# Forward stage of a fused attention and FFN training step: the 64-row part of the products as two 32-row matmuls beside score pairs, and a queue and bank of their own for weight-gradient sums

## The chip, the cores and the metric

One core of one Trainium2 chip runs the whole program in one launch. The metric is the device time of the program in microseconds; the time before is the median of three runs. Instructions of each engine run in their program order: TensorE (matmuls and their weight loads), VectorE, ScalarE, GpSimd and SyncE, the last two also issuing most of the DMAs. What one engine needs of another is waited for by semaphores.

## The reference

A layer of attention and a SwiGLU FFN side by side on the same normalised input, forward, and the gradients of all inputs but one. S = 2048 rows, D = 448, 16 heads of 28, F = 1792, bf16 inputs, batch 1.

```python
def _A_ref(x, wqkv, wo):
    qkv = (x @ wqkv).reshape(B, S, 3, H, Dh).transpose(2, 0, 3, 1, 4)
    q, k, v = qkv[0], qkv[1], qkv[2]
    scores = jnp.einsum("bhqd,bhkd->bhqk", q, k) * (Dh ** -0.5)
    p = _softmax(scores, axis=-1)
    o = jnp.einsum("bhqk,bhkd->bhqd", p, v)
    return o.transpose(0, 2, 1, 3).reshape(B, S, D) @ wo

def _B_ref(x, w_gate, w_up, w_down):
    return (_silu(x @ w_gate) * (x @ w_up)) @ w_down

xn = _layernorm(x, axis=-1)
return x + _A_ref(xn, A_wqkv, A_wo) + _B_ref(xn, B_w_gate, B_w_up, B_w_down)
# outputs: this, and its vjp with grad_out for x and the five weights
```

## The kernel before

It has a prologue, a forward loop, a backward loop and an end.

The prologue normalises x into xn_sp (rows on partitions), transposes it into xnT (four chunks of D on partitions: 128, 128, 128 and 64 rows, the last filled up with zeros), and makes q, k and v of head group 0 (proj_unit, four matmuls each into one bank, evicted with a constant added that sets the spare head columns).

The forward loop has 256 steps (g, qc, kt): head group g of four heads of 32 padded rows, query chunk qc of 512, key tile kt of 128. A step (L517 to L544) has two halves. Each half makes the scores of two heads with two 32-row matmuls into s_ps (L531), at row positions 0 and 32 in the first half, 64 and 96 in the second, and ScalarE takes their exponential into eT (L535). In the second half the four PV matmuls of the step before follow (L511). After each half fill() puts other work of the forward stage on TensorE, from one queue of jobs; pace is what is left in the queue over the steps left, and a half gets 0.45 or 0.55 of it. The costs in the queue are set by hand (MM, MMD).

The queue holds, for each of 14 blocks fc of 128 columns of F and each quarter sc of the rows: the gate product a, the up product u, and dh, the gradient of the product's input, four 512-column matmuls each (L339) into one bank of ps_f. After a ScalarE takes a tanh (L349) and VectorE makes g1 and, in two operations, w (L351 to L356); after u VectorE makes two products (L363, L365) and after dh two more (L373). These go as fT by DMA to hd_d (GpSimd, L378) and transposed into f_sp (SyncE, L375). Between u and dh of the next block stand the three weight-gradient sums of the block before (dW_items, L313): 16 matmuls of 448 columns each into one bank, evicted by VectorE (L319, L323). Other jobs are put at the front of the queue: the projections of the next head group, the layouts of q and k (sp_layouts), and after each (g, qc) o_items: o_raw is copied out by VectorE (L423), transposed on TensorE (tr, L432), scaled (L437 to L440), then dO is made by 16 small matmuls (do, L454) and evicted with its row sums (L461 to L473); after the last qc follow the 16 matmuls of dWo (L400).

All of these take their banks from ps_f, which has three; scores have four and PV one, eight in all. fT has three buffers, f_sp two. weight_layout (L250) transposes weights for backward through the one buffer sp_stage. At step 224 GpSimd issues the load of w_down into the buffer W (load_w, L493), which the projection weights wq_sb share until then.

The backward loop (L772) and the end are not edited. In backward, scores and their gradients are pairs of 32-row matmuls at rows 0 and 32 (L793) and at 64 and 96 (L803), VectorE multiplies (L814) and ScalarE takes exponentials (L808).

Of the kernel before, what the change touches and what calls it, by code (L numbers as in the profile page):

```python
# [37 lines left out]
def kernel(  # L38
# [72 lines left out]
    ps_f = bst.enter_context(tc.tile_pool(name="ps_f", bufs=3, space=PSUM))  # L111
# [15 lines left out]
    pool.memset(xn_sp[:, :, D:], 0.0)  # L127
    pool.memset(wq_sb, 0.0)
    for c, (d0, dn) in enumerate(DCH):
        pool.tensor_copy(  # L130
            out=wq_sb[:dn, c].rearrange("p t g (hh r) -> p t (g hh) r", r=HP)[:, :, :, :DH],
            in_=wst[:dn, c, :].rearrange("p (t h d) -> p t h d", t=3, h=H))
    sp.dma_start(out=dy_sp[:, :, :D], in_=dy_d)
    pool.memset(dy_sp[:, :, D:], 0.0)
# [13 lines left out]
    def proj_unit(g, tq, sc, evac):  # L148

        key = (g, tq)  # L150
        if sc == 0:
            qk_tiles[key] = (vp if tq == 2 else qkp).tile([P, S], BF16, name=("qT", "kT", "vT")[tq])
        dst = qk_tiles[key]
        pp = ps_f.tile([P, 512], FP32, name="f_ps")

        def mm(c):
            pe.matmul(pp[:], lhsT=wq_sb[:, c, tq, g, :], rhs=xnT[:, 4 * sc:4 * sc + 4, c, :],  # L157
                      start=(c == 0), stop=(c == 3))
            if c < 3:
                return  # L160
            o = dst[:, sc * 512:(sc + 1) * 512]
            if tq == 0:
                if evac == "act":
                    act.copy(out=o, in_=pp[:])
                else:
                    dve.tensor_copy(out=o, in_=pp[:])
            elif evac == "act":
                act.activation(out=o, in_=pp[:], func=ACT.Identity, bias=r_ones[:, 0:1], scale=1.0)
            else:
                dve.tensor_scalar(out=o, in0=pp[:], scalar1=r_ones[:, 0:1], scalar2=None, op0=ALU.add)  # L170
        return mm
# [18 lines left out]
    for b in range(5):  # L190
        if b < 4:
# [7 lines left out]
            for i in range(4):  # L199
# [3 lines left out]
                                  op0=ALU.subtract, op1=ALU.mult)  # L203
                pt = ps_s.tile([P, 4, P], BF16, name="s_ps")
# [3 lines left out]
        if b > 0:  # L208
            for tq in range(3):
                m = proj_unit(0, tq, b - 1, "act" if tq == 0 else "dve")  # L210
                for c in range(4):
                    m(c)
    proj_done(0)
# [12 lines left out]
    for w in wgu:  # L226
        pool.memset(w[64:, :, 3, :], 0.0)
    pool.memset(wd3[:, :, 64:], 0.0)
# [3 lines left out]
    def load_ffn_w(fc):  # L232
        w, fs = wgu[fc % 2], slice(fc * P, (fc + 1) * P)
        q = sp if fc < 2 else pool
        for i, src in enumerate((B_w_gate, B_w_up)):
            q.dma_start(out=w[:, i, 0:3, :], in_=src[0:384, fs].rearrange("(c p) f -> p c f", p=P))
            q.dma_start(out=w[:64, i, 3, :], in_=src[384:448, fs])
# [3 lines left out]
    sp.dma_start(out=wd3[:, :, 0:64], in_=B_w_down[:, 384:448].rearrange("(fc p) d -> p fc d", p=P))  # L241
# [20 lines left out]
    queue = deque()  # L262
    cur = deque()
    left = [0.0]

    def fill(budget):

        while budget > 0.05:
            if not cur:
                if not queue:  # L270
                    return
                cur.extend(queue.popleft())
            cost, fn = cur.popleft()
            fn()
            budget -= cost
            left[0] -= cost

    def push(jobs, front=False):
        left[0] += sum(c for job in jobs for c, _ in job)
        if front:  # L280
            queue.extendleft(reversed(jobs))
        else:
            queue.extend(jobs)

    def proj_items(g):
        out = []
        for tq in range(3):
            for sc in range(4):
                box = {}

                def go(c, tq=tq, sc=sc, box=box):
                    if c == 0:
                        box["m"] = proj_unit(g, tq, sc, "dve")
                    box["m"](c)
                out.append([(MM, lambda c=c, go=go: go(c)) for c in range(4)])
        out.append([(0.0, lambda: proj_done(g))])
        return out

    ffn = {}

    def dW_items(fc):

        out = []
        for wi in range(3):
            box = {}

            def go(t, wi=wi, box=box):
                src = ffn[fc]
                if t == 0:
                    box["ps"] = ps_f.tile([P, 512], FP32, name="f_ps")  # L310
# [4 lines left out]
                if t < NT - 1:  # L315
                    return
                if wi == 0:
# [14 lines left out]
    def ffn_items(fc, sc, extra):  # L332
# [3 lines left out]
        def mm(name, w, src, c):  # L336
            if c == 0:
                st[name] = ps_f.tile([P, 512], FP32, name="f_ps")
            pe.matmul(st[name][:], lhsT=w(c), rhs=src[:, tsl, c, :], start=(c == 0), stop=(c == 3))  # L339

        def a(c):
            if c == 0 and sc == 0:
                ffn[fc] = spp.tile([P, 3 * NT, P], BF16, name="f_sp")
                if fc + 1 < NFC:
                    load_ffn_w(fc + 1)
            mm("a", lambda c: wgu[fc % 2][:, 0, c, :], xnT, c)
            if c == 3:
                t_sb = st["t"] = ftmp.tile([P, 512], FP32, name="t_sb")
                act.activation(out=t_sb[:], in_=st["a"][:], func=ACT.Tanh, scale=0.5)  # L349
                g1 = st["g1"] = ftmp.tile([P, 512], FP32, name="g1")  # L350
                dve.scalar_tensor_tensor(out=g1[:], in0=t_sb[:], scalar=1.0, in1=st["a"][:],  # L351
                                         op0=ALU.add, op1=ALU.mult)
                w = st["w"] = ftmp.tile([P, 512], FP32, name="w_sb")
                dve.scalar_tensor_tensor(out=w[:], in0=t_sb[:], scalar=1.0, in1=g1[:],
                                         op0=ALU.subtract, op1=ALU.mult)
                dve.scalar_tensor_tensor(out=w[:], in0=w[:], scalar=-0.5, in1=t_sb[:],  # L356
                                         op0=ALU.mult, op1=ALU.add)

        def u(c):
            mm("u", lambda c: wgu[fc % 2][:, 1, c, :], xnT, c)  # L360
            if c == 3:
                o = st["o"] = fT.tile([P, 3, 512], BF16, name="fT")
                dve.scalar_tensor_tensor(out=o[:, 0, :], in0=st["g1"][:], scalar=0.5, in1=st["u"][:],  # L363
                                         op0=ALU.mult, op1=ALU.mult)
                dve.scalar_tensor_tensor(out=st["w"][:], in0=st["w"][:], scalar=1.0, in1=st["u"][:],  # L365
                                         op0=ALU.add, op1=ALU.mult)

        def dh(c):
            mm("dh", lambda c: wdT[fc % 2][:, c, :], dyT, c)
            if c == 3:  # L370
                o = st["o"]
                for wi, src in ((2, "g1"), (1, "w")):
                    dve.scalar_tensor_tensor(out=o[:, wi, :], in0=st["dh"][:], scalar=0.5, in1=st[src][:],  # L373
                                             op0=ALU.mult, op1=ALU.mult)
                sp.dma_start_transpose(out=ffn[fc][:, 12 * sc:12 * sc + 12, :],  # L375
                                       in_=o[:].rearrange("p w s -> p (w s)"))
                for wi in range(3):
                    pool.dma_start(out=hd_d[tsl, :, G + NFC * wi + fc, :].rearrange("k p s -> p k s"),  # L378
                                   in_=o[:, wi, :].rearrange("p (k s) -> p k s", k=4))

        def four(f):
            return [(MM, lambda c=c: f(c)) for c in range(4)]
        return [four(a), four(u)] + extra + [four(dh)]

    ffn_list = []
    pend = []
    for fc in range(NFC):
        nxt = dW_items(fc)
        for sc in range(4):
            ffn_list += ffn_items(fc, sc, pend[sc - 1:sc] if sc else [])  # L390
        if 0 < fc < 13:
            ffn_list.append([(0.0, lambda k=fc - 1: weight_layout(k // 3, k % 3))])
        pend = nxt
    ffn_list += pend
    push(ffn_list)
# [11 lines left out]
    def dwo_items(g):  # L407
        box = {}

        def go(t):  # L410
            if t == 0:
                box["ps"] = ps_f.tile([P, 512], FP32, name="f_ps")
# [7 lines left out]
    def o_items(g, qc, o_ps):  # L420
# [8 lines left out]
        def tr(i):  # L429
            if i == 0:  # L430
                st["ot"] = ps_f.tile([P, 4, P], FP32, name="f_ps")
# [18 lines left out]
        def do(i):  # L450
            if i == 0:
                st["do"] = ps_f.tile([P, 4, P], FP32, name="f_ps")
# [3 lines left out]
            if i < 3:  # L456
# [23 lines left out]
        push([[(0.2, lambda i=i: tr(i)) for i in range(4)], [(0.26, lambda i=i: do(i)) for i in range(4)]]  # L480
             + (dwo_items(g) if qc == 3 else []), front=True)
# [34 lines left out]

    for i, (g, qc, kt) in enumerate(steps):  # L517
        if kt == 0 and qc == 1:
            push([[(0.0, lambda g=g: sp_layouts(g))]], front=True)
        if kt == 0 and qc == 2 and g + 1 < G:  # L520
            push(proj_items(g + 1), front=True)
# [3 lines left out]
        pace = left[0] / (nst - i)  # L525
        eTs[i] = []
        for half in range(2):
            s_ps = ps_s.tile([P, 2, 512], FP32, name="s_ps")
            for j in range(2):
                r = HP * (2 * half + j)  # L530
                pe.matmul(s_ps[:, j, :], lhsT=kT[r:r + HP, kt * P:(kt + 1) * P],  # L531
                          rhs=qT[r:r + HP, qc * 512:(qc + 1) * 512],
                          start=True, stop=True, tile_position=(r, 0))
            e = ep.tile([P, 2, 512], BF16, name="eT")
            act.activation(out=e[:], in_=s_ps[:], func=ACT.Exp, scale=SCALE)  # L535
            eTs[i].append(e)
            if half == 0:
                fill(0.45 * pace)
            else:
# [4 lines left out]
                fill(0.55 * pace)  # L544
# [3 lines left out]
    fill(1e9)  # L548
# [388 lines left out]
```

## Time and profile before

| what | value |
|---|---|
| runs | 1738.14, 1739.35, 1739.54 us; median 1739.35 |
| the profiled execution, its own time | 1738.91 us |
| its span from the first to the last instruction | 1737.1 us |
| mean granted TensorE clock | 0.954 |
| first score matmul, last forward matmul, first backward matmul | 49.9, 757.7, 765.6 us |
| TensorE busy | 1504.9 us (87%), 12176 matmuls |
| VectorE, ScalarE, GpSimd busy | 1103.0 (63%), 1242.1 (72%), 400.8 us (23%) |

The page cuts the span into 40 slices of 43.4 us with the busy tenths of each engine. A row of a view by stretch gives the stretch, its length, the busy time and number of instructions of each engine, the granted clock, the busy share of the DMA engines and GB/s. A line of the timeline gives start, length, engine, line, operation, what is written and read, the shape and how many are merged; in brackets the idle time before it and what ended it. A line of waits gives who waited for whom, the total, how often and the longest. A matmul's length has its way through the array in it, so that matmuls overlap in these lines; the distance of starts tells the rate.

### The profile page before, as it was taken

How to read it: one execution, taken by the hardware profiler on the slowest of the kernel's cores; microseconds unless marked ns; L12 is line 12 of the kernel's file. 1: busy time of each engine (PE TensorE's matmuls, PEld its weight loads, DVE VectorE, ACT ScalarE, POOL GpSimd, SP SyncE). 2: the span in 40 equal slices, each digit the busy share in tenths (PEclk: the TensorE clock that was granted, in tenths of full speed). 3: DMA queues.
4: the chain of work that ended last, by engine and by line, in shares of the span. 5: the costliest groups of instructions: out<-in, count | busy, mean ns of one | idle time of the engine just before them, and what ended most of it. 6: DMA issues, size and time to landing. Idle time of an engine off the chain costs nothing.

```text
span 1737.1 us, 31931 instructions
## 1 busy us (share of the span) xinstructions
PE 1504.9 (87%) x12176; PEld 590.4 (34%) x12176; DVE 1103.0 (63%) x1402; ACT 1242.1 (72%) x1346; POOL 400.8 (23%) x664
## 2 busy tenths in 40 slices
PE   3799999999999998868888888888888888888885
PEld 2132333333233332223333334333334333433352
DVE  5365555565555454527777767777777777777726
ACT  2497888888777776637777767777777877777711
POOL 4132334343333342420001011110102101111122
PEclk9699999999899999889999989999999999999988
DMA  3794758775866585659999799998999999899873
GB/s 122 149 184 96 160 115 177 142 141 124 173 142 122 106 171 111 135 168 218 202 188 202 143 193 185 178 202 178 205 185 184 209 170 171 156 176 177 168 236 102
DMA packets 682153, 285.11 MB, mean 164 GB/s; under 512 B 637792, under 2 KB 651088, under 8 KB 682000
## 3 DMA queue, kind: packets, MB, share of 16 engines
q1 hardware_dynamic: 653616, 215.74, 65.9%
q0 software_dynamic: 25808, 64.30, 14.6%
q10 hardware_dynamic: 2576, 3.04, 0.6%
q8 instruction: 95, 1.56, 0.4%
q14 instruction: 58, 0.48, 0.1%
HBM read 67.34 MB, written 63.44 MB: 75 GB/s over the span
## 4 chain that ended last, share of the span: by engine, by line
PE 63%; ACT 16%; DMA 6%; DVE 6%; issue 6%; SPq 1%; POOL 1%; ACTq 0%; DVEq 0%; POOLq 0%
PE s_ps L531 9%; PE f_ps L339 9%; PE f_ps L313 8%; ACT E L808 7%; ACT dsT L722 7%; PE aux L664 5%; PE o_ps L511 4%; PE sd L793 4%; PE aux L735 4%; PE aux L658 3%; PE aux L721 3%; PE f_ps L157 3%; PE acc L694 3%; PE sd L803 2%; DMA dsT<-ds 2%
## 5 line engine op out<-in xcount | busy, mean ns | idle before, releaser
L814 DVE TENSOR_TENSOR ds<-sd,E 128x1024 bf16<-128x1024 f32 x512 | 624.3, 1223 | 231.1 <-PE sd L803 209.8
L808 ACT ACTIVATE E<-sd 128x1024 bf16<-128x1024 f32 x512 | 518.5, 1027 | 176.0 <-PE sd L803 153.9
L535 ACT ACTIVATE eT<-s_ps 128x1024 bf16<-128x1024 f32 x512 | 517.9, 1024 | 158.5 <-PE s_ps L531 153.0
L803 PE MATMUL sd<-KV,QD 32*128 32x512 bf16 x1024 | 202.4, 388 | 61.2 <-ACT E L808 60.2
L793 PE MATMUL sd<-KV,QD 32*128 32x512 bf16 x1024 | 201.9, 391 | 7.7 <-DMA KV<-kT_d 7.6
L694 PE MATMUL acc<-E,dOsp 128*32 128x512 bf16 x1024 | 204.4, 396 | 0.6 <-ACT dkv_o L700 0.5
L531 PE MATMUL s_ps<-qT,kT 32*128 32x512 bf16 x1024 | 204.7, 397 | 0.0
L694 PE MATMUL acc<-ds,Qsp 128*32 128x512 bf16 x1024 | 204.6, 396 | 0.0
L722 ACT COPY dsT<-aux 128x1024 bf16<-128x1024 bf16 x128 | 129.5, 1012 | 47.9 <-PE aux L721 46.2
L339 PE MATMUL f_ps<-xnT,wgu 128*128 128x512 bf16 x448 | 137.2, 404 | 24.7 <-DVE w_sb L365 12.9
L378 POOL DMA_DIRECT2D hd_d<-fT x168 | 126.9, 769 | 39.2 <-DVE fT L363 25.4
L531 PEld LDWEIGHTS <-kT 32*128 32x128 bf16 x1024 | 48.3, 91 | 204.2 <-issue 201.9
L664 PE MATMUL aux<-W,ck 128*128 128x448 bf16 x448 | 101.0, 353 | 14.2 <-ACT dsT L722 14.2
L313 PE MATMUL f_ps<-xn_sp,f_sp 128*128 128x448 bf16 x448 | 110.6, 356 | 0.0
L803 PEld LDWEIGHTS <-QD 32*128 32x128 bf16 x1024 | 66.5, 91 | 105.6 <-issue 101.9
L511 PE MATMUL o_ps<-eT,v_sp 128*32 128x512 bf16 x1024 | 102.0, 400 | 0.0
L709 POOL DMA_DIRECT2D dqkv_d<-dkv_o x64 | 39.1, 616 | 271.1 <-ACT dkv_o L700 271.0
L793 PEld LDWEIGHTS <-QD 32*128 32x128 bf16 x1024 | 48.3, 91 | 138.2 <-issue 122.9
L735 PE MATMUL aux<-dsT,Ksp 128*32 128x512 bf16 x1024 | 75.2, 387 | 22.4 <-ACT dsT L722 18.1
L694 PEld LDWEIGHTS <-dOsp 128*32 128x32 bf16 x1024 | 50.7, 93 | 118.8 <-issue 118.7
L721 PE MATMUL aux<-ident_bf,ds 128*128 128x128 bf16 x1024 | 80.3, 222 | 12.3 <-DVE dq_acc L750 6.9
L351 DVE SCALAR_TENSOR_TENSOR g<-t_sb,f_ps 128x512 f32<-128x512 f32 x56 | 38.4, 686 | 65.1 <-ACT t_sb L349 64.9
(129 smaller groups left out, 1731.1 us busy)
## 6 DMA issues: line engine op xcount, KB each, us to landing
hd_d<-fT POOLq DMA_DIRECT2D x168, 128.0 KB, 4.3
ck<-hd_d SPq DMA_DIRECT2D x32, 448.0 KB, 4.2
ck<-hd_d SPq DMA_DIRECT2D x16, 576.0 KB, 4.7
dsT<-ds SPq DMA_TRANSPOSE x384, 3.9
dq_c<-dqkv_d SPq DMA_DIRECT2D x8, 768.0 KB, 4.6
dqkv_d<-dkv_o POOLq DMA_DIRECT2D x64, 64.0 KB, 3.1
W<-wT_d SPq DMA_DIRECT2D x14, 224.0 KB, 3.9
out_dram<-dw_o POOLq DMA_DIRECT2D x28, 96.0 KB, 3.8
```

The lines of the kernel that those rows point to most:

```text
L313: pe.matmul(acc[:, :D], lhsT=src[:, 12 * (t // 4) + 4 * wi + t % 4, :], rhs=rhs[:, t, :D], start=(t == 0), stop=(t == NT - 1))
L339: pe.matmul(st[name][:], lhsT=w(c), rhs=src[:, tsl, c, :], start=(c == 0), stop=(c == 3))
L511: pe.matmul(o_ps[HP * hh:HP * (hh + 1), :], lhsT=v[:, kt, HP * hh:HP * (hh + 1)], rhs=e[hh // 2][:, hh % 2, :], start=(kt == 0), stop=(kt ...
L531: pe.matmul(s_ps[:, j, :], lhsT=kT[r:r + HP, kt * P:(kt + 1) * P], rhs=qT[r:r + HP, qc * 512:(qc + 1) * 512], start=True, stop=True, tile_ ...
L535: act.activation(out=e[:], in_=s_ps[:], func=ACT.Exp, scale=SCALE)
L664: return [lambda n=n: pe.matmul(ps[:, :D], lhsT=t[:, n, :], rhs=w[:, n, :], start=(n == 0), stop=(n == NFC - 1)) for n in range(NFC)]
L694: pe.matmul(acc[r:r + HP, :], lhsT=src[:, qt, 64 * hp + HP * j:64 * hp + HP * j + HP], rhs=m[:, j, :], start=(qt == 0), stop=(qt == NT - 1 ...
L722: act.copy(out=dsT[:, :, :, qi * P:(qi + 1) * P].rearrange("p j c q -> p (j c) q"), in_=ps[:])
L793: pe.matmul(s_ps[:, j, :], lhsT=q[HP * j:HP * j + HP, qt * P:(qt + 1) * P], rhs=kv[HP * j:HP * j + HP, kc * 512:(kc + 1) * 512], start=Tru ...
L803: pe.matmul(d_ps[:, j, :], lhsT=q[r:r + HP, qt * P:(qt + 1) * P], rhs=kv[r:r + HP, kc * 512:(kc + 1) * 512], start=True, stop=True, tile_p ...
L808: act.activation(out=E[k][:], in_=s_ps[:], func=ACT.Exp, scale=SCALE)
L814: dve.tensor_tensor(out=DS[k - 1][:], in0=d_ps[:], in1=E[k - 1][:], op=ALU.mult)
```

## The change

- xn_sp and dy_sp, padded from 448 to 512 columns, hold in the last 64 a second copy of columns 384 to 447 instead of zeros (16 copies on VectorE in the prologue, one on GpSimd for dy_sp); so the fourth chunk of xnT and dyT holds the same 64 rows twice. Weights of the fourth chunk are put in (or, for wq_sb, also in) partitions 64 to 127.
- quad() makes a product of five matmuls: 32 rows at position 64, three of 128 rows, 32 rows at position 96. It is used for FFN products and the projections of groups 1 to 3. The projections of group 0 use four, the last of 64 rows.
- The queue is split: wide holds products, of which a step starts at most one; long_ holds gradient sums, tr, do and dWo. The first 32-row matmul of a product stands beside the first score pair of its step, the three wide ones after it, and the last 32-row matmul beside a score pair of the next step; its eviction follows. Steps that start no product have a small fill in the first half.
- fill() takes from long_ alone, with a credit that is carried on up to 1.5, and ends at the end of a job. The budget is the total of the sums' costs over the steps left after the twelfth.
- Banks: ps_f's three become ps_l (two, products) and ps_d (one, sums, tr and do).
- The sums of a block are queued when its last dh is evicted; f_sp is taken at the first dh, not at the first a.

```diff
@@ pools
-    ps_f = bst.enter_context(tc.tile_pool(name="ps_f", bufs=3, space=PSUM))
+    ps_l = bst.enter_context(tc.tile_pool(name="ps_l", bufs=2, space=PSUM))
+    ps_d = bst.enter_context(tc.tile_pool(name="ps_d", bufs=1, space=PSUM))
@@ prologue
-    pool.memset(xn_sp[:, :, D:], 0.0)
...
+    pool.tensor_copy(out=wq_sb[64:128, 3], in_=wq_sb[0:64, 3])
     sp.dma_start(out=dy_sp[:, :, :D], in_=dy_d)
-    pool.memset(dy_sp[:, :, D:], 0.0)
+    pool.tensor_copy(out=dy_sp[:, :, D:], in_=dy_sp[:, :, D - 64:D])
...
+    def quad(ps, w, src, t0, c):
+        rhs = lambda r, n, ch: src[r:r + n, t0:t0 + 4, ch, :]
+        if c % 4 == 0:
+            r = 64 + 8 * c
+            pe.matmul(ps[:], lhsT=w[r:r + HP, 3, :], rhs=rhs(r, HP, 3), start=(c == 0), stop=(c == 4),
+                      tile_position=(r, 0))
+        else:
+            pe.matmul(ps[:], lhsT=w[:, c - 1, :], rhs=rhs(0, P, c - 1), start=False, stop=False)
...
+                dve.tensor_copy(out=xn_sp[:, t, D:], in_=xn_sp[:, t, D - 64:D])
@@ FFN weights
-    for w in wgu:
-        pool.memset(w[64:, :, 3, :], 0.0)
-    pool.memset(wd3[:, :, 64:], 0.0)
+    pool.memset(wd3[:, :, :64], 0.0)
@@ queues
+    def next_wide():
+        other = []
+        while wide and callable(wide[0]):
+            other.append(wide.popleft())
+        return (wide.popleft()[1]() if wide else None), other
+
+    def step_long():
+        if not cur:
+            cur.extend(long_.popleft())
+        cost, fn = cur.popleft()
+        fn()
+        return cost
+
     def fill(budget):
-        while budget > 0.05:
...
+        credit[0] += budget
+        while credit[0] > 0.05 and (cur or long_):
+            credit[0] -= step_long()
             if not cur:
-                if not queue:
...
+                break
+        credit[0] = min(credit[0], 1.5)
@@ gradient sums, tr, do, dWo
-                    box["ps"] = ps_f.tile([P, 512], FP32, name="f_ps")
+                    box["ps"] = ps_d.tile([P, 512], FP32, name="d_ps")
@@ dh's eviction
+            if sc == 0:
+                while fc >= 2 and dw_done[0] < 3 * (fc - 1):
+                    step_long()
                 ffn[fc] = spp.tile([P, 3 * NT, P], BF16, name="f_sp")
...
+            if sc == 3:
+                long_.extend(dW_items(fc))
@@ the lists
+    n_wide = 3 * 4 * NFC + 12 * (G - 1)
+    long_cost = MMD * NT * (3 * NFC + G) + 4 * G * (4 * 0.2 + 4 * 0.26)
@@ the step
-        pace = left[0] / (nst - i)
+        prev, job, other = job, None, []
+        if begun < max(min(i + 1, 16), 16 + (i - 15) * (n_wide - 16) / 222):
+            job, other = next_wide()
+            begun += 1
         for half in range(2):
             s_ps = ps_s.tile([P, 2, 512], FP32, name="s_ps")
             for j in range(2):
+                if job and not prev and half == 0 and j == 1:
+                    job[0](0)
                 r = HP * (2 * half + j)
                 pe.matmul(s_ps[:, j, :], ...)
+            if job and prev and half == 0:
+                job[0](0)
+            if prev and half == (0 if job else 1):
+                prev[0](4)
             e = ep.tile([P, 2, 512], BF16, name="eT")
             act.activation(out=e[:], in_=s_ps[:], func=ACT.Exp, scale=SCALE)
             eTs[i].append(e)
+            if prev and half == (0 if job else 1):
+                prev[1]()
+            if (half == 0) == bool(job):
+                for f in other:
+                    f()
             if half == 0:
-                fill(0.45 * pace)
+                if job:
+                    for c in range(1, 4):
+                        job[0](c)
+                else:
+                    fill(0.3)
             else:
...
-                fill(0.55 * pace)
+                fill(long_cost / (nst - 12) if i >= 12 else 0.0)
```

## The prediction

> **What bounds it now.** I read the page's slices first, then busy times by stretch, then the timeline, last the waits. Slices 2 to 16 are the forward loop, the only stage that the change edits:
>
> ```profile
> PE   3799999999999998868888888888888888888885
> DVE  5365555565555454527777767777777777777726
> ACT  2497888888777776637777767777777877777711
> PEclk9699999999899999889999989999999999999988
> ```
>
> TensorE is full there and ScalarE near it. By stretch (columns: PE, PEld, DVE, ACT, POOL busy, granted clock, DMA):
>
> ```profile
> 223.60:300.90 77.30, 77.30 (x482) 24.95 (x481) 45.21 (x80) 67.76 (x72) 25.80 (x40) 1.00 0.71 139
> ...
> 557.50:564.40 6.90, 5.43 (x29) 2.93 (x29) 3.73 (x9) 2.05 (x2) 4.99 (x7) 0.51 0.84 177
> ...
> 690.70:707.70 17.00, 7.72 (x24) 1.81 (x23) 5.66 (x9) 2.80 (x3) 12.50 (x17) 0.50 0.87 233
> ```
>
> Quiet stretches have no gap on TensorE. But six stretches of half clock, 58 us together, follow waits of it. A quiet step in the timeline:
>
> ```profile
> 300.89 0.39 PE L531 MATMUL s_ps<-qT,kT 32*128 32x512 bf16 x2
> 301.21 0.74 PE L313 MATMUL f_ps<-dy_sp,f_sp 128*128 128x448 bf16 x3
> 301.88 0.39 PE L531 MATMUL s_ps<-qT,kT 32*128 32x512 bf16 x2
> 302.20 0.40 PE L511 MATMUL o_ps<-eT,v_sp 128*32 128x512 bf16 x4
> 302.53 0.93 PE L313 MATMUL f_ps<-dy_sp,f_sp 128*128 128x448 bf16 x4
> ```
>
> A gradient matmul costs 0.19 us ((0.93 - 0.35)/3), a 512-column product 0.216 (three take 0.82 and one 0.38), a score pair or a set of four PV matmuls 0.32, that is 0.22 and 0.10 for the change of shape. Each of the 256 steps (g, qc, kt) is such a sum: with these prices the 16 steps from 300.9 come to 38.9 us against 39.3 observed. So order and counts give TensorE's time, and waits come on top. The first line below is from the timeline, the others from the totals of waits, of TensorE and of GpSimd:
>
> ```profile
> 147.14 0.55 PE L432 MATMUL f_ps<-ident_f,o_raw 128*128 128x128 f32 x3 [1.81 <-DVE o_raw L423]
> ...
> PE f_ps L339 <- DVE w_sb L365: 12.9, 2, 12.8
> PE f_ps L432 <- DVE o_raw L423: 10.3, 6, 3.2
> PE f_ps L313 <- DMA f_sp<-fT: 2.4, 1, 2.4
> ...
> POOL W L493 <- DMA sp_stage<-W: 31.1, 1, 31.1
> ```
>
> From the starts of the steps' first score matmuls, what they took above the pace beside them, cold stretch included: at four o_raw waits 4.2, 4.8, 5.4 and 6.7 us (21), at the 12.8 us wait 16, at the f_sp wait 7.
>
> **Fewer matmuls.** 204 jobs (168 FFN products, 36 projections of groups 1 to 3) go from four 512-column matmuls to three and two of 32 rows: 204 x 0.216 = -44. Are the 32-row ones free beside a score pair? Backward has four row tiles together:
>
> ```profile
> 1109.25 0.39 PE L793 MATMUL sd<-KV,QD 32*128 32x512 bf16 x2
> ...
> 1109.26 0.39 PE L803 MATMUL sd<-KV,QD 32*128 32x512 bf16 x2
> ...
> 1109.58 0.39 PE L694 MATMUL acc<-E,dOsp 128*32 128x512 bf16 x2
> ```
>
> Four take 0.33 where a pair takes 0.32, with weights of their own: free but for 0.01 x 165. [...] In the changed order of instructions the shape changes 1198 times on TensorE instead of 1265: -7. Together -49.
>
> **Steps that ScalarE bounds.** Two exponentials of 1.024 us (L535) and a third of a tanh of 0.59 (L349) make 2.25 us a step. The new schedule starts one job a step and gives gradient sums a fixed allowance, so some steps run dry: four (0.32), three products (0.74), pair and PV (0.32 each) make 1.70. The order has 27 such steps (the first twelve, and after steps 46, 114 and 173), 0.55 lost in each, and eight nearly empty (the last five among them), 1.5 each: +27; 20 to 30 by how ScalarE averages over neighbours.
>
> **Two banks for products.** (T is a step's start, times in us after it.) A job's first 32-row matmul is queued behind the release of the bank used two jobs before; everything after it on TensorE waits too: three products, a score pair and with it the next exponential, PV. The gate product holds its bank longest. Its last 32 rows go with the scores of the next step at T. The exponential starts at T+0.49 (685.43 to 685.92 in the timeline), ends 1.51, tanh 2.10, g1 (0.69) 2.82, free for TensorE at 2.87. The next step starts at T+2.50 (0.32 + 0.74 + 0.32 + 0.32 + 0.80 with 3.65 gradient matmuls), so it waits 0.37. VectorE then runs w twice (0.72 apart) and the two up products (0.60 apart), frees the second bank at T+5.50, wanted at 5.37: 0.13. A gradient eviction (0.62) between adds 0.15 on average. Of 56 triples four are in the start and five in dry steps; 47 x 0.65 = 31; 20 of the steps without a job fall where they remove 0.5: +21. Bounds 5 (VectorE early) and 31.
>
> **One bank for sums, transposes and dO.** Before, three shared banks let TensorE run on. Now a sum, the transposes and dO each wait for VectorE's reads of the one before, behind FFN work in VectorE's queue. Worked along the order at the block end at step 64: transposes right after o_raw wait 0.9, dO 0.1, dWo for dOl (prod, delta, dOl: 0.60, 0.72, 0.69 after w) 1.45, the next up bank 0.9: 3 us over the usual. At step 128: 4, one wait of 3.2 in it. Blocks in projection steps, with 0.75 of VectorE a job, 0.5 to 1.4. Mean 2 over 15: +30; bounds 12 (VectorE free each time) and 50.
>
> **Half clock.** A wait of 1.81 us before 147.14 was answered by 6.9 us at clock 0.51; of those at least 3 us are lost. The same working finds five waits over 2.3 us (blocks at 48, 96, 128, 192, 208): +15; bounds 0 and 34 (ten). [...]
>
> **Taken away.** The o_raw waits stand in the two terms above: -21. The 31 us stop of GpSimd's queue at L493 ends: W's load stood in front of hd_d stores and waited for a transpose issued 27 us later; in the new order the last weight layout is directly before it. The fT tiles then come free and the 16 go: -16 (bound 0, if the 1.6 MB load itself holds the stores).
>
> **Small things.** Sixteen 64-column copies on VectorE, one 1536-column copy and a wait for dy_sp on GpSimd lie in the prologue, where VectorE, TensorE and ScalarE take turns (gaps of 4 to 5 us each): +2 (0 to 5); the wgu fill that goes hides nothing there worth more than 0.5. At the tail dO waits 1.3 for the single bank, and the backward loads are behind it: +2. Moved DMAs: the next block's weights (four on SP or GpSimd, two transposes on SP), a weight layout (a transpose on SP, a store on GpSimd) and the group layouts (two of each) are issued at the start of a job, no longer between fillers. They have the rest of the block's twelve jobs (some 35 us) to land, against 2.8 to 8.5 us from issue to landing for L493, so I cost them at nothing; if that cover is gone, f_sp transposes stand behind them on SP, as in the 7 us stall, which I keep: bounds -7 and +5. Gradient sums can now start in the step in which the last f_sp transpose is issued; their first 12 matmuls use older ones, which is 7.5 us at 3.65 a step.
>
> **Sum.** -49 + 27 + 21 + 30 + 15 - 37 + 4 = +11 on the execution of 1738.91 (span 1737.1), 0.4 under the median: 1750.
>
> **Rivals.** (1) Faster: VectorE keeps up and two banks suffice. For it: it is busy 45 of 77 us, and dry steps let it catch up. Against: g1 cannot start before T+2.13 even if idle. With the low bounds (20 for dry steps, 5, 12, 0) the sum is -49 + 37 - 37 + 4 = -45, 1694; I put it half way from the forecast, at 1722. It decides once bank waits fall below about 0.15 us a job. (2) The terms cancel: within 0.2%, 1736 to 1743, about what a measurement can tell from no change. For it: the terms are seven of both signs. (3) Half clock feeds itself: each cold stretch delays VectorE's inputs and makes the next wait; ten waits (34) with 45 and 31 for the banks: -49 + 27 + 31 + 45 + 34 - 37 + 4 = +55, 1794. Against: a cold stretch lets VectorE catch up. (4) The small matmuls don't run together, so the change doesn't do what it says: 408 x 0.216 = 88 more, 1838; against it the backward row.
>
> **Numbers.** The forecast (own range 1743 to 1768) 0.47, rival 1 0.29, rival 2 0.12, rival 3 0.10, rival 4 0.02. So faster 0.29, same 0.12, slower 0.59. A range of 1718 to 1785 leaves out some 0.11 below and 0.07 above.
>
> **What would show it.** Right: four matmuls within 0.02 us in forward; new waits of l_ps on g1 (some 40) and of d_ps on dOl and o_raw; ScalarE without gaps in dry steps; more than six half-clock stretches; no long GpSimd wait at W. Wrong: l_ps waits under 5 us in total (then rival 1), fours that take over 0.4 us (rival 4), or a backward stage whose length moved.

## The result and the profile after

The changed kernel takes 1768.05 us (median of six runs, 1762.9 to 1771.92) against 1738.74 for six runs of the kernel before beside it: 1.0175 times as long, 95% interval 1.0153 to 1.0198. Medians and ratios leave out executions in a slower state of the chip; only the last experiment had any, three of twelve. The forecast was 1750, slower: the direction held, but the cost is +29 instead of +11, at the upper edge of the forecast's own range (1743 to 1768). The profiled execution took 1771.92 (span 1770.1, mean granted TensorE clock 0.947), 33 more than the one before.

The busy tenths of the page for the changed kernel; slices 2 to 18 are the forward loop:

```profile
PE   3689899998998899977888888888888888888875
...
DVE  6365456545554555415777776777777777777726
ACT  2477678777787677756777776777777778777711
...
PEclk8899899989999899978999989999999999999988
```

TensorE's nines have become eights, VectorE's and ScalarE's digits have fallen too: no engine took over as the bound. The core waits more. From the starts of the steps' first score matmuls, with the prediction's prices for what each step holds (0.2155 us for 512 columns, 0.19 for a gradient matmul, 0.10 for each change of shape; besides 0.05 for a matmul of dO, where 16 take 1.00 with one change of shape, and 0.2 for a transpose, the kernel's own cost, where four take 0.59 with one: some 0.12 each, as many before as after; 32-row matmuls beside scores are priced as free):

| part of the span, us | before | after | difference | forecast |
|---|---|---|---|---|
| work of the 255 step distances, by prices | 625.5 | 574.6 | -50.9 | -49 |
| up to the first score, first five steps, last step to the first backward matmul | 86.2 | 92.0 | +5.8 | +4 |
| steps with under 1.95 us of work and no more than 3 us long ("dry"), above the price | 0.0 | 24.4 | +24.4 | +27 |
| other steps above the price: waits and half clock | 54.0 | 106.4 | +52.4 | +29 |
| backward, from its first matmul to its last | 955.8 | 956.1 | +0.3 | 0 |

The sum is +32; the last 1 us lies behind the last matmul. Forecast for the fourth row: 21 + 30 + 15 - 37. A product in a quiet place of the timeline:

```profile
139.55 0.39 PE L547 MATMUL s_ps<-qT,kT 32*128 32x512 bf16 x2
139.56 0.39 PE L155 MATMUL l_ps<-xnT,wgu 32*128 32x512 bf16 x2
139.88 0.82 PE L158 MATMUL l_ps<-xnT,wgu 128*128 128x512 bf16 x3
```

Two scores and two 32-row matmuls (a four) start within 0.01 us and the next group starts 0.33 later: they are free, as forecast. Two things stand beside this. In the 34 steps that start no product, the last 32-row matmul (row position 96) stands beside the second score pair, which is at rows 64 and 96 itself:

```profile
127.34 0.39 PE L547 MATMUL s_ps<-qT,kT 32*128 32x512 bf16 x2
127.57 0.37 PE L155 MATMUL l_ps<-xnT,wgu 32*128 32x512 bf16 x1
127.88 0.40 PE L521 MATMUL o_ps<-eT,v_sp 128*32 128x512 bf16 x4
```

It starts 0.23 late and the three take 0.54 where a pair takes 0.32 (24 of the 34 take 0.53 or 0.54, four in half clock 0.96 or 0.97): these 34 cost what they would have cost as 128-row matmuls, 34 x 0.215 = 7 us, which the first row of the table counts as saved and the third and fourth contain. And a four can wait for its bank without any idle time in the profile, since the score pair's own length of 0.39 covers the wait:

```profile
271.59 0.39 PE L547 MATMUL s_ps<-qT,kT 32*128 32x512 bf16 x2
271.96 0.37 PE L155 MATMUL l_ps<-dyT,wdT 32*128 32x512 bf16 x1
271.96 0.38 PE L155 MATMUL l_ps<-xnT,wgu 32*128 32x512 bf16 x1
272.28 0.82 PE L158 MATMUL l_ps<-dyT,wdT 128*128 128x512 bf16 x3
```

VectorE's g, which reads the bank that is wanted, ends at 271.91; the 32-row matmuls start 0.05 later, and this four takes 0.69 instead of 0.33. What TensorE waits for between 80 and 790 us (total, times, longest), and below it GpSimd's wait at the load of W:

```profile
PE d_ps L441 <- DVE o_raw L432: 13.1, 8, 4.4
PE d_ps L409 <- DVE dOl L476: 6.3, 3, 3.0
PE l_ps L155 <- DVE w_sb L373: 5.8, 13, 0.6
PE l_ps L155 <- DVE g L361: 5.7, 8, 0.8
PE d_ps L327 <- DMA f_sp<-fT: 5.5, 2, 3.0
PE d_ps L441 <- DVE dwT L338: 4.6, 2, 2.5
...
POOL W L503 <- issue: 0.2, 1, 0.2
```

The 31 us stop at W and the 12.8 us wait behind it are gone. In their place stand many waits for VectorE, 14.0 us for product banks (l_ps) and 38.3 in front of what uses the single bank (d_ps, without f_sp; 13.1 of it is for o_raw, an input). The longest, at step 192, unfolds in the timeline of all engines:

```profile
599.75 3.07 ACT L555 ACTIVATE eT<-s_ps 128x1024 bf16<-128x1024 f32 x3 [0.30 <-PE s_ps L547]
...
601.06 0.37 PE L155 MATMUL l_ps<-xnT,wgu 32*128 32x512 bf16 x1
...
601.36 0.40 PE L521 MATMUL o_ps<-eT,v_sp 128*32 128x512 bf16 x4
...
602.71 0.60 ACT L359 ACTIVATE t_sb<-l_ps 128x512 f32<-128x512 f32 x1
603.35 0.69 DVE L361 SCALAR_TENSOR_TENSOR g<-t_sb,l_ps 128x512 f32<-128x512 f32 x1 [2.22 <-ACT t_sb L359]
...
605.40 0.68 DVE L432 COPY o_raw<-o_ps 128x512 f32<-128x512 f32 x1
...
606.14 0.69 PE L441 MATMUL d_ps<-ident_f,o_raw 128*128 128x128 f32 x2 [4.38 <-DVE o_raw L432]
```

Read it backwards. The transposes wait 4.38 us for o_raw. Its source o_ps was complete at 601.76, but the copy starts at 605.40, since VectorE's queue has g and both w in front of it, and g stands 2.22 us, idle, for the tanh. The gate product was complete at 601.43; the tanh starts at 602.71, behind an exponential that stands before it in ScalarE's order.

### The profile page after: what moved, and what is told of

Read it like the earlier page. It is cut to its first block, busy times and chain, and to the rows that moved or that the text cites. A ratio compares the mean times of both kernels' runs of the same rounds, so it can differ in the third digit from the quotient of the medians.

```text
span 1770.1 us, 32356 instructions
## 1 busy us (share of the span) xinstructions
PE 1501.1 (85%) x12380; PEld 588.0 (33%) x12380; DVE 1103.7 (62%) x1418; ACT 1235.0 (70%) x1346; POOL 401.2 (23%) x662
## 4 chain that ended last, share of the span: by engine, by line
PE 54%; ACT 18%; DVE 11%; issue 7%; DMA 7%; SPq 1%; POOL 1%; ACTq 0%; DVEq 0%; POOLq 0%
PE d_ps L327 7%; ACT E L839 7%; ACT dsT L753 7%; PE s_ps L547 6%; PE l_ps L158 6%; PE aux L695 5%; PE sd L824 4%; PE aux L766 4%; PE aux L689 3%; PE o_ps L521 3%; PE aux L752 3%; PE acc L725 3%; PE sd L834 2%; ACT eT L555 2%; DMA dsT<-ds 2%
## 5 line engine op out<-in xcount | busy, mean ns | idle before, releaser
L361 DVE SCALAR_TENSOR_TENSOR g<-t_sb,l_ps 128x512 f32<-128x512 f32 x56 | 38.5, 687 | 164.2 <-ACT t_sb L359 164.2
L327 PE MATMUL d_ps<-xn_sp,f_sp 128*128 128x448 bf16 x448 | 110.2, 361 | 7.7 <-DVE dwd_sb L334 3.1
L158 PE MATMUL l_ps<-xnT,wgu 128*128 128x512 bf16 x336 | 96.3, 397 | 0.0
L766 PE MATMUL aux<-dsT,Ksp 128*32 128x512 bf16 x1024 | 75.2, 387 | 20.2 <-ACT dsT L753 18.3
```

What stands on the lines that cost most here:

```text
L158: pe.matmul(ps[:], lhsT=w[:, c - 1, :], rhs=rhs(0, P, c - 1), start=False, stop=False)
L327: pe.matmul(acc[:, :D], lhsT=src[:, 12 * (t // 4) + 4 * wi + t % 4, :], rhs=rhs[:, t, :D], start=(t == 0), stop=(t == NT - 1))
```

## The experiments

Ratios are against the kernel before on the same chip; differences are between medians. Of TensorE's time, "falls" counts how often between 80 and 750 us its granted clock went from full to half; before 6, after 13. The next table splits the time above the price (third and fourth row together, the steps from the sixth on) for four kernels, two of them experiments below. Half clock is half of TensorE's busy time in half-clock stretches; late fours are what fours took above 0.33 us without idle time. All figures are rounded.

| us in these steps | before | after | tanh first | four products |
|---|---|---|---|---|
| above the price | 54 | 131 | 98 | 88 |
| idle before products | 13 | 15 | 9 | 13 |
| idle before sums, transposes and dO | 10 | 35 | 27 | 34 |
| idle for f_sp | 3 | 6 | 4 | 3 |
| idle before scores (ScalarE) | 0 | 5 | 8 | 6 |
| late fours | none | 19 | 7 | none |
| last 32-row matmul at row 96 | none | 7 | 7 | none |
| half clock | 23 | 35 | 25 | 23 |
| the rest | 4 | 10 | 11 | 10 |

**Is it the place of the tanh?** The eviction of the product (tanh, then VectorE's work) is put ahead of the half's exponential.

```diff
-            act.activation(out=e[:], in_=s_ps[:], func=ACT.Exp, scale=SCALE)
-            eTs[i].append(e)
             if prev and half == (0 if job else 1):
                 prev[1]()
+            act.activation(out=e[:], in_=s_ps[:], func=ACT.Exp, scale=SCALE)
+            eTs[i].append(e)
```

> The changed kernel with the eviction of the step before put in front of the first half's exponential, so the tanh no longer stands behind 1.02 us of exponential. Theory two banks: the gate's bank is free about 1 us earlier, the waits of L155 on g and w_sb (11.5 us shown, more hidden below 0.4 us each) go: -12 us (-5 to -20). Rival: ScalarE is as full as TensorE, and the late exponential delays score pairs: 0 to +10.

Measured 1738.63 (ten runs), 0.9989 (0.9971 to 1.0008): -29, the whole loss, more than the range allowed. VectorE's row for g, of the page after and of this run (busy, mean ns, idle before and what ended it):

```profile
L361 DVE SCALAR_TENSOR_TENSOR g<-t_sb,l_ps 128x512 f32<-128x512 f32 x56 | 38.5, 687 | 164.2 <-ACT t_sb L359 164.2
```

```profile
L361 DVE SCALAR_TENSOR_TENSOR g<-t_sb,l_ps 128x512 f32<-128x512 f32 x56 | 38.5, 687 | 117.9 <-ACT t_sb L359 117.9
```

VectorE stands 46 us less in front of g (before: 65.1). The fourth row of the first table falls from 106.4 to 77.6, dry steps from 24.4 to 20.2. So the late tanh costs 29 us. Two ways lead from it to TensorE: sum, transpose and dO evictions stand behind g in VectorE's queue, or the gate's product bank is held longer. The table shows both: idle time before products and late fours fall by 18 us together, idle time before sums, transposes and dO by 8, half clock by 10. To which way the half clock belongs isn't shown; no run has only VectorE's three gate operations moved.

**Are the 32-row matmuls worth anything?** Products as four 128-row matmuls, in the new queues and banks.

```diff
-        rhs = lambda r, n, ch: src[r:r + n, t0:t0 + 4, ch, :]
...
+        for ch in {1: [0], 2: [1], 3: [2, 3]}.get(c, []):
+            pe.matmul(ps[:], lhsT=w[:, ch, :], rhs=src[:, t0:t0 + 4, ch, :], start=(ch == 0), stop=(ch == 3))
```

> The changed kernel without the two 32-row matmuls: four 512-column matmuls of 128 rows again, all in the job's own step, queues, banks and pacing as changed. The 64-row part of the projections of groups 1 to 3 is counted twice, so q, k and v of these groups are other values. If the 32-row matmuls are free beside score pairs: 204 x 0.216 = +44 us of matmuls, less some 20 of waits for the two product banks that fall away since a job's first matmul stands 0.3 us later: +15 to +35. Rival small matmuls (they cost what they save): -10 to +5.

Measured 1771.25, 1.0178 (1.0163 to 1.0193): +3 only, inside the spread of the changed kernel's runs. The number alone would fit the rival; the rows above don't, for 170 of the 204 products. The steps' work is 44 us more by prices (618.6), and the time above the price falls by 43: late fours 19, half clock 12 (falls from 13 to 8, mean granted clock 0.957 against 0.947), the matmuls at row 96 7, idle time 5. So of the 44 us 7 were never saved, and the other 37 come back as waits for banks and half clock. The same edit on the version with the tanh first:

> The tanh-first kernel (1738.6 us) without the two 32-row matmuls: four 128-row matmuls in the job's own step, as in the run before that gave only +3 on the changed kernel (same part counted twice, so q, k and v of groups 1 to 3 are other values). Theory gate chain (in the changed kernel the step's length is set by exponential, tanh, g1 and the bank, so TensorE's count doesn't show; with the tanh first it does): +25 to +40 us over tanh-first, 1764 to 1779. Rival small matmuls (they cost what they save): -5 to +8.

Measured 1751.15, 1.0099 (1.0074 to 1.0124): +12.5 over the tanh-first version by the medians, some 19 by the ratios: between the two theories either way. Where VectorE is less late, more of the 37 us shows, a third to a half.

**What does the split of the banks cost alone?** The kernel before with ps_l (two) for products, ps_d (one) for sums, transposes and dO.

```diff
-    ps_f = bst.enter_context(tc.tile_pool(name="ps_f", bufs=3, space=PSUM))
+    ps_l = bst.enter_context(tc.tile_pool(name="ps_l", bufs=2, space=PSUM))
+    ps_d = bst.enter_context(tc.tile_pool(name="ps_d", bufs=1, space=PSUM))
```

> The kernel before, with only its three shared banks split as in the change: two for products, one for sums, transposes, dO and dWo; order, queue and matmuls as before. Theory one bank: dO now waits for VectorE's reads of the transposes (1.3 us and what stands before them), each sum for the eviction of the one before, fifteen blocks and 42 sums with some cold stretches behind: +20 us (+8 to +40). Rival gate chain (the bank split matters only in the new order, where each step starts a product): 0 to +5.

Measured 1806.88, 1.0405 (1.0378 to 1.0432): +71, far over what was expected. In the steps from the sixth on TensorE's idle time goes from 26 to 70 us, half clock from 23 to 39. TensorE's waits, first lines:

```profile
PE l_ps L340 <- DVE w_sb L366: 23.7, 13, 14.9
PE d_ps L455 <- DVE O_sp L441: 20.1, 15, 2.5
PE d_ps L433 <- DVE o_raw L424: 9.6, 6, 3.0
```

The new second line is dO waiting for the transposes' bank at nearly every block end, since the old order puts dO directly behind them. The falls go from 6 to 12 (mean granted clock 0.943 against 0.954). The longest wait, 14.9, is the one behind W's load. The way from here to the change: the new queues, still with four matmuls, take 36 back (1771.25), the end of the stop at W included; the 32-row matmuls take 3 more (1768.05).

**W's load, and transposes held back.** Two edits of the kernel before. First, load_w("wd") issued directly behind the last weight layout:

```diff
+        if (c, i) == (3, 2):
+            load_w("wd", 1)[0]()
...
-        if kt == 0 and qc == 2 and g + 1 == G:
-            load_w("wd", 1)[0]()
```

> The kernel before, with the load of w_down moved from step 224 to directly behind the last weight layout; nothing else. The prediction's term: GpSimd's stop of 31 us at L493 ends and with it the 12.8 us wait of TensorE and its cold stretch, -16 us, near 1723. Rival: the 1.6 MB load itself holds the hd_d stores wherever it stands, then 0 to -5.

Measured 1724.21, 0.9915 (0.9894 to 0.9935): -15. The prediction's -16 for this move stands. Then, in the changed kernel, o_items' jobs held for two steps, so that o_raw is ready when the transposes come:

```diff
-        long_.extendleft(reversed([[(0.2, lambda i=i: tr(i)) for i in range(4)],
-                                   [(0.26, lambda i=i: do(i)) for i in range(4)]]
-                                  + (dwo_items(g) if qc == 3 else [])))
+        held.append((now[0] + 2, [[(0.2, lambda i=i: tr(i)) for i in range(4)],
+                                  [(0.26, lambda i=i: do(i)) for i in range(4)]]
+                     + (dwo_items(g) if qc == 3 else [])))
...
+        now[0] = i
+        while held and held[0][0] <= i:
+            long_.extendleft(reversed(held.pop(0)[1]))
```

> The changed kernel, with transposes, dO and dWo queued two steps after the copy of o_raw instead of at once. Theory one bank (TensorE's waits for VectorE's reads of d_ps and o_raw, and the half clock behind them, are what the change gives away): the o_raw waits with their cold stretches were some 30 us over the steps' content, a few come back elsewhere: -20 us (-12 to -28). Rival dry steps (the half clock comes of steps in which TensorE has too little to do): -5 to +3, as the fillers only move.

Measured 1758.75, 1.0109 (1.009 to 1.0128): -9, less than the range allowed. On the tanh-first version:

> Tanh-first with transposes, dO and dWo queued two steps after the copy of o_raw. Theory one bank: the o_raw waits left (11 us shown, with cold stretches some 18) mostly go, part comes back at dOl and sums, as the deferral alone gave -9: -8 us (-3 to -14), near 1730. Rival: VectorE is early enough once the tanh is first: 0.

Measured 1731.91 (ten runs), 0.9975 (0.9954 to 0.9997): -7 by the medians, but only -2 by the ratios, whose intervals overlap, so that a gain isn't clear. And both edits on the kernel before, with its three shared banks:

> The kernel before, with the load of w_down behind the last layout (1724.2 us alone) and the transposes queued two steps after o_raw. The four o_raw waits with their cold stretches were 21 us: -15 more, near 1709 (1703 to 1717). Rival: they move to other waits, as half of the deferral did on the changed kernel: 1717 to 1724.

Measured 1700.58, 0.979 (0.9767 to 0.9813): faster than both kernels and under its range, 35 us under the kernel before beside it (1735.5) and some 67 under the changed one. Its waits of TensorE, between 80 and 752 us:

```profile
PE f_ps L341 <- DVE w_sb L367: 6.0, 4, 3.1
...
PE f_ps L435 <- DVE o_raw L426: 0.9, 1, 0.9
PE f_ps L315 <- DMA f_sp<-fT: 0.6, 1, 0.6
```

Of 26 us of such waits 7.5 are left, of 6 falls 3 (mean granted clock 0.967). Holding back is worth about 24 with three banks and 9 with one (22 and 11 by the ratios). What the split of the banks would cost in this order no run shows.

**The credit.** Two waits for f_sp (5.5 us) come where a carried credit lets many sum matmuls into one step. Cap 0.2 in place of 1.5:

```diff
-        credit[0] = min(credit[0], 1.5)
+        credit[0] = min(credit[0], 0.2)
```

> The changed kernel with the credit's cap at 0.2 instead of 1.5, so that a step never takes twelve sum matmuls at once. The waits for f_sp at steps 54 and 182 with their cold stretches were 11 us: -8 (-3 to -12). Rival: the cold stretches move on to the next wait for VectorE: 0.

Measured 1769.03, 1.0192 (1.0158 to 1.0226): nothing, as the rival said. The waits for f_sp go, those for dOl, w_sb and g grow, and there are 12 falls, in other places (mean granted clock 0.953 against 0.947).

**Projections mixed with FFN products** (tanh first), so that VectorE's heavy triples are spread:

```diff
-            wide.extendleft(reversed(proj_items(g + 1)))
+            mixed = []
+            for item in proj_items(g + 1):
+                mixed.append(item)
+                while not callable(item) and wide:
+                    mixed.append(wide.popleft())
+                    if not callable(mixed[-1]):
+                        break
+            wide.extendleft(reversed(mixed))
```

> Tanh-first with each projection of the next group followed by one FFN product instead of twelve projections in a row. Theory dry steps (the sums' queue runs empty while projections run, some 18 us over the content): -6 us (-12 to 0). Rival: sums are short in total, dry steps only move: -2 to +3.

Measured 1742.12 (ten runs), 1.002 (1.0003 to 1.0038): +3.5, a miss; the reason wasn't followed. All of it together, with the credit's cap of 0.2, sums from step 14, what is left of them spread over the last steps, and an empty item behind dO:

```diff
+    def rest(i):
+        late = sum(c for job_ in long_ for c, _ in job_) + sum(c for c, _ in cur)
+        return max(0.0, late / (2 * (nst - i)) - credit[0] / 4)
...
-                                  [(0.26, lambda i=i: do(i)) for i in range(4)]]
+                                  [(0.26, lambda i=i: do(i)) for i in range(4)],
+                                   [(0.6, lambda: None)]]
...
-                fill(long_cost / (nst - 12) if i >= 12 else 0.0)
+                fill(rest(i) if not (wide or prev or job) else long_cost / (nst - 12) if i >= 14 else 0.0)
```

> Tanh-first, deferral, mixed projections, the credit's cap 0.2 instead of 1.5 (no twelve sums in one step), sums from step 14, an empty item of 0.6 behind dO, and what is left of the sums spread over the last 18 steps. Added up: -8 (o_raw), -5 (f_sp), -6 (dOl), -4 (tail), -4 (dry steps) from 1738.6: 1711 (1703 to 1725). If the one bank only moves its waits about, 1730 or more.

Measured 1725.58, 0.9942 (0.9925 to 0.9959): faster than before, just outside the range. The same without the mixing, and with an empty item behind the transposes:

> As the kernel that had everything (1725.6 us), without the mixed projections, which gave nothing alone, and with an empty item behind the transposes too, so that dO starts a step later: the 7.7 us of waits on O_sp and their cold stretches go: 1718 (1713 to 1724). If the waits only move: 1725.

Measured 1726.67 (nine runs), 0.9946 (0.9927 to 0.9966): no better, as its rival said. The new scheme, so mended, does not reach the old one with its two edits.

## Why the prediction was right in direction and short in size

- **Fewer matmuls, -49: right by prices** (-50.9). In 170 of the 204 products both small matmuls stand beside a pair at other rows; a four that waits for nothing takes 0.33 against 0.32 (93 of the 165 in the trace; what the later ones take above it is in the table under late fours, idle before products and half clock). The other 34 put the last 32 rows at the row position of a score, which the forecast put at nothing: 7 us. Rival 4 is out for the 170.
- **Dry steps, +27: right** in size (+24.4; the first five steps, which the forecast counted here, are in the second row). Only 4 of it shows as TensorE waiting for ScalarE itself; 10 are waits for a product bank, behind tanh and g.
- **Taken away at W, -16: right** (-15 alone).
- **Start and tail, +4:** +5.8. **Backward:** unmoved, as forecast. (The forward loop before reaches into slice 18, not 16; no term rests on it.)
- **Half clock, 15: here it failed.** The forecast's fourth row comes to 83 us (54 and 29), the measured one to 106. Half clock is 32 of these, where the forecast had 15 and some 3 in the f_sp stall that it kept: 14 of the 23 that are missing. It counted waits over 2.3 us and found five; the clock fell 13 times, eleven times at a single wait of 1.46 to 4.38 us and twice at two waits in one window (1.02 and part of 2.12; 0.82 and part of 0.54; last section). Cold stretches at TensorE's waits came as forecast; the count by waits over 2.3 us was wrong.
- **Two banks 21, one bank 30: nearly right.** In the fourth row the product banks take 24 (9 idle, 15 in late fours), the single bank 34. The working named a wait of 4.4 us at step 192, and 4.38 stands there. It followed o_raw, dO and dOl through block ends, but gave no time to a sum or the transposes that wait for the sum before them to be evicted (waits for dwd_sb and dwT, 10.7 us). The rest of the 23 is the matmuls at row 96 (4 in this row) and what is left over.
- The chain "exponential, tanh, g1" that the term **Two banks** wrote down was the right one; it was only charged to the product banks. It also delays what stands behind g in VectorE's queue: moving the tanh alone was worth 29, and 8 of the waits that went were for the single bank's work.
- Rival 3 (half clock feeds itself, ten waits, 34) had the size of the half clock and, with 13, nearly the count of falls, but its banks were too dear (76 against 58). The credit run shows its trait, that a stall taken away comes back elsewhere. Rival 1 (VectorE keeps up, 1722) did not come even with the tanh first (1738.63), and rival 2 (the terms cancel, 1736 to 1743) is 25 us away.

## What to carry to other kernels

Before work is taken off the engine that looks full, find who releases its banks: once its inputs and banks come from another engine's in-order queue, some 37 us of saved matmuls were worth 3, and 12 to 19 once that queue was less late. Follow that queue to its first waiting instruction; here one tanh behind an exponential held the evictions queued behind it, and its place was worth 29 us. Check the row positions too: the small matmuls were free beside scores at other row positions (0.33 us against 0.32), and 34 that stood at the position of a score cost their full time (0.54). Stops that a trace already shows (a load issued too early, transposes queued right behind the copy that they need) are cheaper gains: two small edits gave 35 us.

## What the runs showed of the chip

In the traces of the two kernels all changes of the granted clock (33 before, 47 after) lie on one grid of 3.413 us in each, to within 0.003. Between 80 and 750 us the falls go with the idle time of TensorE summed over such a window rather than with single waits. Four windows of the changed kernel in a row (stretch, length, busy PE, PEld, DVE, ACT, POOL, granted clock, DMA), and two waits from its timeline:

```profile
191.14:194.56 3.42, 1.88 (x15) 0.50 (x13) 2.30 (x4) 3.42 (x5) 0.05 (x1) 1.00 1.05 183
194.56:197.97 3.41, 1.79 (x8) 0.95 (x9) 2.13 (x6) 0.38 (x2) 0.00 (x0) 0.50 1.16 206
197.97:201.39 3.42, 3.42 (x21) 1.88 (x19) 0.56 (x1) 2.02 (x2) 0.00 (x0) 0.50 0.91 235
201.39:204.80 3.41, 2.45 (x21) 0.62 (x20) 3.06 (x8) 2.75 (x3) 0.18 (x1) 1.00 0.16 39
```

```profile
193.13 0.39 PE L547 MATMUL s_ps<-qT,kT 32*128 32x512 bf16 x2 [1.02 <-ACT eT L555]
...
205.54 0.39 PE L155 MATMUL l_ps<-xnT,wgu 32*128 32x512 bf16 x2 [1.70 <-DVE fT L383]
```

In the first window TensorE is idle for 1.54 us: 1.02 in a dry step, the rest the beginning of the wait for o_raw that follows. The second is at half clock and, idle for 1.62, is followed by another; that one is busy, and the fourth is at full clock again. The wait of 1.70 at its end is cut in two by the grid (0.96 idle in this window) and no half clock follows (the next window, from 204.80, has 0.74 idle and granted clock 1.00). In the two traces, between 80 and 750 us, 19 full-clock windows were followed by half clock; 18 of them had 1.46 to 3.41 us idle and one 1.20 (waits of 0.82 and 0.54 from 406.03 on). The 333 others, with at most 1.31, were followed by full clock. Of 38 half-clock windows the 12 with 0.39 to 3.41 us idle were followed by another one; of the 26 without idle time 19 were followed by full clock. So dry steps weren't free even where ScalarE bounded them: in the window from 191.14 the 1.02 of one made up 1.54 with the first 0.52 of the next wait, and half clock followed. Full-clock windows with 0.51 to 1.31 us idle number 1 before and 23 after.
